# PE transposes for the first tile of each batch, the first two tiles in lockstep, and a fixed step table for attention from tile 4 on

## The chip, the cores and the metric

The kernel runs on one core of a Trainium2 chip. The core has TensorE (PE, matmuls, with PEld for the loading of weights into the array), VectorE (DVE), ScalarE (ACT), GpSimd (POOL) and SyncE (SP, which here issues every DMA), 16 DMA engines, the on-chip memory SBUF, and PSUM, where TensorE leaves its results. The metric is device time of one execution in microseconds (us). Three runs of the kernel before took 695.65, 696.09 and 697.74 us; their median is 696.09.

## The reference

Four batches of 768 tokens, 8 heads of 64. Attention sees the first 8 keys of a sequence (global) and the last 96 (local); a feed-forward block with layer norm follows, and its input is added to its output.

```python
scores = scale * np.matmul(q, k.transpose(0, 1, 3, 2))
is_global = pos[None, :] < int(n_global)
is_local = (rel >= 0) & (rel < int(n_local))
dist = np.where(is_global & ~is_local, float(n_local), np.abs(rel))
scores = np.where(is_global | is_local, scores - slopes * dist, -1e9)
a = np.exp(scores - max); a = a / (a.sum() + 1e-9)
x = np.matmul(a, v)                        # then (4, 768, 512)
xn = (x - mu) / np.sqrt(var + 1e-06) * g_ln
out = x + np.maximum(xn @ w_ch1, 0.0) @ w_ch2
```

The two weight matrices are 512x2048 and 2048x512, and they lie in memory as eight-byte floating-point words.

## The kernel before

**Numbers in two halves.** A value in four bytes is split into a high and a low two-byte half; a product is summed from three matmuls (high by high, high by low, low by high), scores from all four halves' products. `ffn1` (L330 to L332) and `product2` (L344) show it, and so do the three matmuls of pv (L259 to L261). The eight-byte weights are turned into two halves on the chip by `weight` (L144 to L157): three ACT and three DVE operations for each of 16 pieces of 1 MB, with three `st` buffers for the pieces.

**Tiles.** The 3072 tokens are 24 tiles of 128 tokens. `TILES` (L49) puts the first tile of each batch ahead: tiles 0 to 3 are first tiles of batches 3, 2, 1, 0; tiles 4 to 8 the rest of batch 0, and so on. A first tile attends only to itself (one block of 128 keys); any other attends to itself and the block ahead of it, into whose first 16 columns the global keys are copied (L215, L216). Two tiles form a chunk for the feed-forward part (`CT` = 2, twelve chunks).

**One tile's attention** (`attention`, L190) is a Python generator; its `yield`s are the places where other work may be traced in between. k, q and v are loaded into `ld` buffers (six of them) and split into halves. k (L180) and q (L202) are transposed by DMA; the halves of q change places for the cross products (L208; by DVE copies for tile 0, L206). Then come scores `s` (L234), masking with a row minimum (L239), the exponential (L243), the split of the result into `pn` (L246 on ACT for tiles 0 to 3, L248 on DVE after that, and L249 on POOL), its transpose by DMA (L251, `pT`, three buffers), pv with v (L259 to L261), the division (L265), the norm (`norm`, L269 to L282) and a last DMA transpose into `xT` (L282).

**PSUM.** Four pools of two banks: scores (`ps_s`), pv (`ps_v`), ffn1 (`ps_1`) and ffn2 (`ps_2`, tag `f2`).

**What sets the order.** The order on each engine is planned at compile time. The planner knows the data dependences and estimated durations; program order is the priority. `ORDER` and `mk` add some fixed edges by hand: a mark in the table waits in program order for another. Tile 0 is traced first, with the masks inside it; `run(f1w(), tokens(1), 0.6)` converts the first weight matrix, runs ffn1 of tile 0 alone (128 columns wide) and lets tile 1's generator advance 0.6 yields for each of its own. Tiles 1 to 3 follow likewise. Then `run(ffn(c), side, RATE)` goes through the chunks: for each step of the feed-forward part of chunk c, 1.6 yields of the attention of later tiles (`side`), one tile after another, up to one tile (`AHEAD`) past chunk c + 1.

Of the kernel before, what the change touches and what calls it, by code (L numbers as in the profile page):

```python
# [75 lines left out]
def banded(ctx, tc, q, k, v, n_global, n_local, g_ln, w1, w2, out, flag):  # L76
# [35 lines left out]

    def piece(src, name):
        st = p3.tile([P, 2, 512], I64, tag="st", name="st" + name, bufs=3)
        mk("D" + name, load.dma_start(out=st, in_=src))
# [28 lines left out]
    def weight(st, dh, dl, name, n):  # L144
# [6 lines left out]
        mk("A" + name, act.activation(out=lo, in_=st.rearrange("p a n -> p (a n)").bitcast(U32).rearrange("p (n two) -> p n two", two=2)[:, :, 0], func=AF.Relu, scale=2.0 ** -29, bias=less))  # L151
# [522 lines left out]
```

## Time and profile before

| what | value |
|---|---|
| median of three runs | 696.09 us (695.65 to 697.74) |
| span of the profiled execution, first to last instruction | 697.8 us |
| instructions | 14209 |
| PE busy, share of the span | 596.8 us, 86% |
| DVE busy | 392.7 us, 56% |
| ACT busy | 291.9 us, 42% |
| POOL busy | 157.5 us, 23% |
| DMA: moved, mean rate | 93.30 MB, 134 GB/s |
| mean granted clock of TensorE | 0.971 |

The profiled execution has no time of its own beside its span; the three runs above are what it can be held against. Rows of a group read: line, engine, operation, output<-input by the program's names, partitions x elements and type, count | busy us, mean ns of one | idle time of the engine just before, and what ended most of it. Rows of busy time by stretch read: the stretch and its length, then for PE and PEld (or all five engines) busy us and the number of instructions, then the granted clock of TensorE, the busy share of the DMA engines and GB/s. Rows of waits read: engine, waiting output and line <- what it waited for: us in total, times, longest. Timeline rows start with start and duration. SPq is the queue of DMA issues.

### The profile page before, as it was taken

The page shows a single profiled execution, that of the slowest core. Times are in us where ns is not written, and L with a number is a line of the kernel's source. Part 1 is how long each engine was busy: PE and PEld are TensorE (multiplying, and loading weights), DVE is VectorE, ACT ScalarE, POOL GpSimd, SP SyncE. Part 2 cuts the span into 40 slices and gives each one's busy share as a digit, 9 for nine tenths or more (in the row PEclk, how much of TensorE's full clock was granted, in tenths as well). Part 3 has the DMA queues.
Part 4 walks back from the last instruction along what each step waited for, and adds up shares of the span by engine and source line. Part 5 has one row for each costly group of instructions (what it writes and reads, how often), then busy time and mean ns, then how long its engine had stood idle before and what let it go on. Part 6 is the DMA issues. An engine that isn't in the chain of part 4 may idle for free. (4 is left out here: it accounts for less than half of the span.)

```text
span 697.8 us, 14209 instructions
## 1 busy us (share of the span) xinstructions
PE 596.8 (86%) x5602; PEld 426.6 (61%) x5602; DVE 392.7 (56%) x976; ACT 291.9 (42%) x752; POOL 157.5 (23%) x141
## 2 busy tenths in 40 slices
PE   0107698998499988999999999899989999999995
PEld 0106576775377576587496586496576586694762
DVE  4887978725567777565456456365445456342111
ACT  4886959323424442354254254253243254140110
POOL 0111304213213313332221331222231232120000
PEclk9999799999599999999999999999999999999999
DMA  9999999936888766676948746856853855231001
GB/s 230 221 278 262 237 260 187 172 58 115 163 161 143 129 139 136 134 148 117 178 90 151 140 96 134 150 106 123 159 118 73 151 82 94 69 62 31 16 1 36
DMA packets 264731, 93.30 MB, mean 134 GB/s; under 512 B 254416, under 2 KB 254416, under 8 KB 264656
## 3 DMA queue, kind: packets, MB, share of 16 engines
q1 hardware_dynamic: 264656, 92.31, 65.2%
q8 instruction: 46, 0.75, 0.5%
q14 instruction: 29, 0.24, 0.1%
HBM read 37.23 MB, written 6.29 MB: 62 GB/s over the span
## 5 line engine op out<-in xcount | busy, mean ns | idle before, releaser
L344 PE MATMUL f<-w2h,h_None 128*128 128x512 f16 x640 | 197.0, 380 | 0.0
L330 PE MATMUL f_None<-xT,w1h 128*128 128x256 f16 x640 | 176.1, 275 | 2.9 <-DVE h_None L336 2.4
L331 PE MATMUL f_None<-xT,w1h 128*128 128x256 f16 x640 | 176.1, 275 | 0.0
L332 PE MATMUL f_None<-xT,w1l 128*128 128x256 f16 x640 | 175.9, 275 | 0.0
L249 POOL TENSOR_TENSOR pn<-T,pn 128x512 f16<-128x512 f32 x88 | 109.2, 1243 | 218.2 <-DVE pn L248 111.6
L344 PEld LDWEIGHTS <-h_None 128*128 128x128 f16 x960 | 91.9, 98 | 99.7 <-issue 1.6
L344 PE MATMUL f<-w2l,h_None 128*128 128x512 f16 x320 | 121.8, 381 | 0.0
L331 PEld LDWEIGHTS <-w1h 128*128 128x128 f16 x896 | 90.7, 101 | 28.6 <-issue 19.0
L330 PEld LDWEIGHTS <-w1h 128*128 128x128 f16 x896 | 90.8, 101 | 16.5 <-DMA xT<-xn 6.9
L332 PEld LDWEIGHTS <-w1l 128*128 128x128 f16 x896 | 90.8, 101 | 7.6
L243 ACT ACTIVATE T<-T,mn 128x256 f32<-128x256 f32 (+1 forms) x192 | 92.4, 484 | 3.6
L335 ACT ACTIVATE h_None<-f_None 128x512 f16<-128x512 f32 x80 | 47.2, 592 | 107.1 <-PE f_None L332 107.0
L336 DVE SCALAR_TENSOR_TENSOR h_None<-f_None,h_None 128x512 f16<-128x512 f32 x80 | 54.7, 684 | 50.8 <-ACT h_None L335 50.8
L239 DVE CUSTOM_DVE_ANT_0 T<-s,mask 128x256 f32<-128x256 f32 (+1 forms) x192 | 67.1, 396 | 25.5 <-PE s L234 25.0
L234 PE MATMUL s<-kT,qT 128*128 128x128 f16 x704 | 55.2, 226 | 25.5 <-DMA qT<-qn 14.2
L259 PE MATMUL pv<-vn,pT 128*128 128x64 f16 x352 | 40.9, 196 | 39.9 <-DMA pT<-pn 39.8
L234 PEld LDWEIGHTS <-qT 128*128 128x128 f16 x704 | 47.4, 101 | 34.6 <-DMA qT<-qn 14.3
L330 PE MATMUL f<-xT,w1h 128*128 128x128 f16 x256 | 50.4, 237 | 17.1 <-DMA xT<-xn 17.1
L248 DVE CAST pn<-T 128x512 f16<-128x512 f32 x80 | 39.9, 502 | 42.8 <-ACT T L243 39.0
L259 PEld LDWEIGHTS <-pT 128*128 128x128 f16 x352 | 32.4, 99 | 50.1 <-DMA pT<-pn 47.9
L178 POOL TENSOR_TENSOR kn<-kf,kn 128x512 f16<-128x512 f32 x20 | 25.5, 1273 | 121.0 <-ACT kn L177 121.0
L276 POOL TENSOR_TENSOR rs<-rs,half 128x1 f32<-128x1 f32 x24 | 22.4, 931 | 133.5 <-DVE rs L275 133.5
(96 smaller groups left out, 804.0 us busy)
## 6 DMA issues: line engine op xcount, KB each, us to landing
st<-in_moe_w_ch_dram SPq DMA_DIRECT2D x16, 1024.0 KB, 7.4
vf<-in_v_dram SPq DMA_DIRECT2D x27, 256.0 KB, 3.6
kf<-in_k_dram SPq DMA_DIRECT2D x26, 256.0 KB, 3.8
qf<-in_q_dram SPq DMA_DIRECT2D x24, 256.0 KB, 3.3
out_dram<-x SPq DMA_DIRECT2D x24, 256.0 KB, 2.4
qT<-qT SPq DMA_DIRECT2D x46, 128.0 KB, 2.4
pT<-pn SPq DMA_TRANSPOSE x88, 3.3
kT<-kn SPq DMA_TRANSPOSE x27, 4.1
```

The costliest lines, as they stand in the source:

```text
L234: last = chain(last, pe.matmul(ps[:, u, n_ * P:(n_ + 1) * P], lhsT=qT[:, a * H + h, :], rhs=use[n_][0][:, h, :], start=(a == 0), stop=(a = ...
L239: vec.tensor_tensor_reduce(out=T[:, u, :], in0=ps[:, u], in1=mask, scale=1.0 / Z, scalar=3e38, op0=ALU.add, op1=ALU.min, accum_out=nm[:, h ...
L243: mk(f"e{t}_{g}", act.activation(out=T[:, u, :], in_=T[:, u, :], func=AF.Exp, scale=-1.0, bias=mn[:, h:h + 1], accum_out=sm[:, h:h + 1]))
L248: vec.tensor_copy(out=pn[:, :, 0, :], in_=T)
L249: pool.tensor_tensor(out=pn[:, :, 1, :], in0=T, in1=pn[:, :, 0, :], op=ALU.subtract)
L259: last = chain(last, pe.matmul(pv[:, h, :], lhsT=ph, rhs=vv[:, h, :D], start=(n_ == 0), stop=False))
L330: last = chain(last, pe.matmul(ps[:, a], lhsT=w1h[:, kk, fs], rhs=xT[:, kk, cols], start=(kk == 0), stop=False))
L331: last = chain(last, pe.matmul(ps[:, a], lhsT=w1h[:, kk, fs], rhs=xT[:, NK + kk, cols], start=False, stop=False))
L332: last = chain(last, pe.matmul(ps[:, a], lhsT=w1l[:, kk, fs], rhs=xT[:, kk, cols], start=False, stop=(kk == NK - 1)))
L335: mk("h" + key, act.activation(out=hh[:, 0], in_=ps, func=AF.Relu))
L336: mk("l" + key, vec.scalar_tensor_tensor(out=hh[:, 1], in0=ps, scalar=0.0, in1=hh[:, 0], op0=ALU.max, op1=ALU.subtract))
L344: pe.matmul(ps, lhsT=hh[:, a, :], rhs=w, start=(f == 0 and n_ == 0), stop=(f == NF - 1 and n_ == 2))
```

## The change

A new generator `first` does tiles 0 to 3. k and q stay in four-byte words as loaded; TensorE transposes them in four pieces of 128x128 against an identity matrix into a bank of `ps_2` (`flip`), and ACT and DVE split the result into halves straight out of PSUM (`split`). The same is done with the exponentials ahead of pv and with the normed x ahead of `xT`, so that no DMA transposes stand in these tiles. Heads 2j and 2j+1 share a transposed piece, in its upper and lower 64 partitions, and scores are taken over 64 partitions with four matmuls a head. The keys of a batch's first tile are loaded and transposed by DMA once more where tile 1 of the batch needs them, for all four batches now.

Tiles 0 and 1 are traced in lockstep (`pair`), with all six loads at the very start, and then tiles 2 and 3 in lockstep with the conversion of the first weight matrix and ffn1 of chunk 0. ffn1 is always 256 columns wide. ffn1 of chunk 1 is traced with the conversion of the second matrix, then ffn2 of tiles 0 and 1, then of 2 and 3.

From tile 4 on a table takes the place of the rate: `begin` gives each tile a step, eight steps from tile to tile, and `step` is called once for each step of the feed-forward part. A tile loads k, q and v in its step 0, splits and transposes q in 2, swaps q's halves in 4, takes scores in 6, 8, 10 and 12, and pv `LAG` = 4 steps after its scores, in 10, 12, 14 and 16. Two tiles are under way at a time. The hand-made edges (`ORDER`, `mk`) are gone. `pT` has four buffers instead of three; `mask0` and the identity matrix take `h` buffers.

```diff
-AHEAD = 1
-RATE = 1.6
+STEP = 8
+LAG = 4
...
-ORDER = {"D1_0_1": "q0", "L1": "q0", "L2": "p0_1", "L3": "p1_1"}
-ORDER.update({f"X{n}": f"l{2 + n // 8}_{2 * n % 16}" for n in range(16)})
...
-    early = {name: fetch(src, name, *TILES[0]) for name, src in (("k", k), ("q", q))}
+    early = {(name, t): fetch(src, name, *TILES[t]) for t in range(CT) for name, src in (("k", k), ("q", q), ("v", v))}
...
-    mask0 = const.tile([P, H, P], BF16, name="mask0")
+    mask0 = hpool.tile([P, H, P], BF16, tag="h", name="mask0")
     mask1 = const.tile([P, H, 2, P], BF16, name="mask1")
+    ident = hpool.tile([P, P], F32, tag="h", name="eye")
+    make_identity(nc, ident)
...
-        (pool if i else vec).tensor_tensor(out=kn[:, :, D:], in0=kf, in1=kn[:, :, :D], op=ALU.subtract)
+        pool.tensor_tensor(out=kn[:, :, D:], in0=kf, in1=kn[:, :, :D], op=ALU.subtract)
...
+    def flip(src, name):
+        ps = ps_2.tile([P, 4, P], F32, tag="f2", name=name)
+        for j in range(4):
+            pe.transpose(ps[:, j, :], src[:, j * P:(j + 1) * P], ident)
+        return ps
+    def split(ps, hi, lo, scale):
+        act.activation(out=hi, in_=ps, func=AF.Copy, scale=scale)
+        if scale == 1.0:
+            vec.tensor_tensor(out=lo, in0=ps, in1=hi, op=ALU.subtract)
+        else:
+            vec.scalar_tensor_tensor(out=lo, in0=ps, scalar=scale, in1=hi, op0=ALU.mult, op1=ALU.subtract)
+    def smalls():
+        return [p2.tile([P, H], F32, name=n_) for n_ in ("nm", "mn", "sm", "r")]
+    def row(pv, vv, h, n_, nb, ph, pl, last):
+        last = chain(last, pe.matmul(pv[:, h, :], lhsT=ph, rhs=vv[:, h, :D], start=(n_ == 0), stop=False))
+        last = chain(last, pe.matmul(pv[:, h, :], lhsT=ph, rhs=vv[:, h, D:], start=False, stop=False))
+        return chain(last, pe.matmul(pv[:, h, :], lhsT=pl, rhs=vv[:, h, :D], start=False, stop=(n_ == nb - 1)))
+    def quotient(pv, sm, r, x):
+        vec.tensor_scalar(out=r, in0=sm, scalar1=PS * 1e-9, scalar2=VS, op0=ALU.add, op1=ALU.mult)
+        vec.reciprocal(out=r, in_=r)
+        vec.tensor_tensor(out=x, in0=pv, in1=r.unsqueeze(2).to_broadcast([P, H, D]), op=ALU.mult)
+    def first(t, x, xT, at):
+        b, _ = TILES[t]
+        raw = [early[name, t] if (name, t) in early else fetch(src, name, b, 0) for name, src in (("k", k), ("q", q), ("v", v))]
+        yield
+        sides = []
+        for src, name, scale in ((raw[0], "k", 1.0), (raw[1], "q", -QS)):
+            d = p2.tile([P, 2, 4, P], F16, tag="kT0" if name == "k" else "qT", name=f"{name}0_{t}")
+            split(flip(src.rearrange("p h d -> p (h d)"), f"{name}t{t}"), d[:, 0], d[:, 1], scale)
+            sides.append(d)
+        kT, qT = sides
+        yield
+        vn = values(b, 0, raw[2])
+        firsts[b] = vn
+        nm, mn, sm, r = smalls()
+        parts = []
+        for e in range(2):
+            yield
+            T = p2.tile([P, 4, P], F32, tag="T", name=f"T{t}_{e}", bufs=3)
+            ps = ps_s.tile([P, 4, P], F32, tag="s", name=f"s{t}_{e}")
+            side = slice(e * D, (e + 1) * D)
+            last = None
+            for j in range(4):
+                for n_, (a, c) in enumerate(((0, 0), (0, 1), (1, 0), (1, 1))):
+                    last = chain(last, pe.matmul(ps[:, j, :], lhsT=qT[side, a, j, :], rhs=kT[side, c, j, :], start=(n_ == 0), stop=(n_ == 3)))
+            for j in range(4):
+                h = 2 * j + e
+                vec.tensor_tensor_reduce(out=T[:, j, :], in0=ps[:, j], in1=mask0[:, h], scale=1.0 / Z, scalar=3e38, op0=ALU.add, op1=ALU.min, accum_out=nm[:, h:h + 1])
+            act.activation(out=mn[:, e::2], in_=nm[:, e::2], func=AF.Copy, bias=LN_PS)
+            for j in range(4):
+                h = 2 * j + e
+                act.activation(out=T[:, j, :], in_=T[:, j, :], func=AF.Exp, scale=-1.0, bias=mn[:, h:h + 1], accum_out=sm[:, h:h + 1])
+            parts.append(T)
+        last = None
+        for e, T in enumerate(parts):
+            yield
+            pT = p2.tile([P, 2, 4, P], F16, tag="pT", name=f"pT{t}_{e}", bufs=LAG)
+            split(flip(T.rearrange("p j w -> p (j w)"), f"pt{t}_{e}"), pT[:, 0], pT[:, 1], 1.0)
+            if e == 0:
+                pv = ps_v.tile([P, H, D], F32, tag="pv", name=f"pv{t}")
+            for j in range(4):
+                last = row(pv, vn, 2 * j + e, 0, 1, pT[:, 0, j, :], pT[:, 1, j, :], last)
+        yield
+        quotient(pv, sm, r, x)
+        rs = moments(t, x)
+        xs = p2.tile([P, DM], F32, tag="T", name=f"xs{t}", bufs=3)
+        vec.tensor_scalar(out=xs, in0=x.rearrange("p h d -> p (h d)"), scalar1=mv[:, t, 0:1], scalar2=rs, op0=ALU.subtract, op1=ALU.mult)
+        vec.tensor_mul(out=xs, in0=xs, in1=gb)
+        yield
+        cols = slice(at * P, (at + 1) * P)
+        split(flip(xs, f"xt{t}"), xT[:, :NK, cols], xT[:, NK:, cols], 1.0)
+    firsts = {}
...
-        if i == 1 and b:
-            blocks[b, 0] = keys(b, 0), values(b, 0)
-            yield
         kT = keys(b, i)
-        qf = early["q"] if t == 0 else fetch(q, "q", b, i)
-        yield
+        qf = fetch(q, "q", b, i)
+        vf = fetch(v, "v", b, i)
+        if i == 1:
+            blocks[b, 0] = keys(b, 0), (firsts[b] if b == 0 else values(b, 0))
+        yield 2
         qn = p2.tile([P, H, P], F16, tag="ld", name=f"qn{t}", bufs=6)
         act.activation(out=qn[:, :, :D], in_=qf, func=AF.Copy, scale=-QS)
         vec.scalar_tensor_tensor(out=qn[:, :, D:], in0=qf, scalar=-QS, in1=qn[:, :, :D], op0=ALU.mult, op1=ALU.subtract)
         qT = p2.tile([P, 2 * H, P], F16, name="qT")
-        mk(f"q{t}", sp.dma_start_transpose(out=qT[:, :H, :], in_=qn.rearrange("p h d -> p (h d)")))
-        yield
+        sp.dma_start_transpose(out=qT[:, :H, :], in_=qn.rearrange("p h d -> p (h d)"))
+        vn = values(b, i, vf)
+        blocks[b, i] = kT, vn
+        yield 4
         for here, there in ((slice(0, D), slice(D, P)), (slice(D, P), slice(0, D))):
-            if t == 0:
-                vec.tensor_copy(out=qT[here, H:, :], in_=qT[there, :H, :])
-            else:
-                load.dma_start(out=qT[here, H:, :], in_=qT[there, :H, :])
-        yield
-        vn = values(b, i)
-        blocks[b, i] = kT, vn
+            load.dma_start(out=qT[here, H:, :], in_=qT[there, :H, :])
+        yield 6
...
+        pTs, last, pv = {}, None, None
+        for step in range(6, 13 + LAG):
+            if i > 1 and step == 5 + LAG:
+                vec.tensor_copy(out=vp[:GK], in_=vg[:GK])
+            g, odd = divmod(step - 6, 2)
+            if not odd and g < H // gh:
+                T = p2.tile([P, gh, W], F32, tag="T", name=f"T{t}_{g}", bufs=3)
+                ps = ps_s.tile([P, gh, W], F32, tag="s", name=f"s{t}_{g}")
...
+                pTs[g] = p2.tile([P, gh * 2 * nb, P], F16, tag="pT", name=f"pT{t}_{g}", bufs=LAG)
+                sp.dma_start_transpose(out=pTs[g], in_=pn.rearrange("p j a w -> p (j a w)"))
+            g, odd = divmod(step - 6 - LAG, 2)
+            if not odd and g >= 0:
+                pT = pTs.pop(g)
+                for u in range(gh):
+                    h = g * gh + u
+                    if h == 0:
+                        pv = ps_v.tile([P, H, D], F32, tag="pv", name=f"pv{t}")
+                    for n_ in range(nb):
+                        last = row(pv, use[n_][1], h, n_, nb, pT[:, (u * 2) * nb + n_, :], pT[:, (u * 2 + 1) * nb + n_, :], last)
+            yield step + 1
+        quotient(pv, sm, r, x)
...
-        yield from attention(t, xs[t], xTs[c], at)
+        yield from (attention if TILES[t][1] else first)(t, xs[t], xTs[c], at)
...
-    def ffn1(c, f, t=None):
-        n, cols = (CT * P, slice(0, CT * P)) if t is None else (P, slice(t % CT * P, (t % CT + 1) * P))
+    def ffn1(c, f):
+        n = CT * P
...
-            if f % 4 == 3 and f < NF - 1:
+            if (f + 1) * len(ts) % 4 == 0 and f < NF - 1:
...
+    def ffn_due(j, c_):
+        if c_:
+            ffn1(0, 4 * j)
+            ffn1(0, 4 * j + 2)
...
-    one = tokens(0)
-    for _ in range(4):
-        next(one)
-    build_masks()
-    go(one)
-    build_mask1()
-    run(f1w(), tokens(1), 0.6)
-    run(f1(1), tokens(2), 2.0)
-    run(f1(2), tokens(3), 2.0)
-    run(f2w(), f1(3), 0.5)
...
-    run(seq(ffn2(0, 1), ffn2(2), ffn2(3)), side(3 * CT + AHEAD), RATE)
-    for c in range(2, NC):
-        g = side((c + 2) * CT + AHEAD)
-        run(ffn(c), extremes(g) if c == 3 else g, RATE)
...
+    pair = both(tokens(0), tokens(1))
+    next(pair)
+    build_masks()
+    go(pair)
+    build_mask1()
+    begin = {t: 7 * (t - 2 * CT) if t < 6 else STEP * (t - 7) + 23 for t in range(2 * CT, B * NT)}
+    live, now, t_next = [], 0, 2 * CT
+    def step():
+        nonlocal now, t_next
+        while t_next in begin and begin[t_next] <= now:
+            live.append([now, t_next, tokens(t_next)])
+            t_next += 1
+        for g in list(live):
+            while g[0] <= now:
+                at = next(g[2], None)
+                if at is None:
+                    live.remove(g)
+                    break
+                g[0] = begin[g[1]] + at
+        now += 1
+    def run(main, *others):
+        for _ in main:
+            step()
+            for g in others:
+                next(g, None)
+    half1 = both(f1w(), tokens(2), tokens(3))
+    go(itertools.islice(half1, 4))
+    run(half1)
+    run(blocks1(1), f2w())
+    run(ffn2(0, 1))
+    run(ffn2(2, 3))
+    run(ffn(2))
+    run(ffn(3), extremes())
+    for c in range(4, NC):
+        run(ffn(c))
```

`smalls`, `row`, `quotient` and `moments` hold lines of the old `attention` and `norm` unchanged.

More of the change, by code (lines that the diff above doesn't have):

```diff
@@ L160, in weights1 @@
         sl, cs = slice(j * 512, (j + 1) * 512), slice(2 * c, 2 * c + 2)
-        weight(piece1(j, c) if j or c else early["w"], w1h[:, cs, sl], w1l[:, cs, sl], f"1_{j}_{c}", 2 * j + c)
+        weight(piece1(j, c), w1h[:, cs, sl], w1l[:, cs, sl], f"1_{j}_{c}", 2 * j + c)
     def weights2(f):
@@ L215, in attention @@
             vec.tensor_copy(out=kp[:, :, :GK], in_=kg[:, :, :GK])
-            vec.tensor_copy(out=vp[:GK], in_=vg[:GK])
-        use = [blocks[b, j] for j in range(max(i - 1, 0), i + 1)]
-        nb = len(use)
+        use = [blocks[b, i - 1], blocks[b, i]]
+        nb, gh = 2, 2
         W = nb * P
-        gh = 4 // nb
-        nm = p2.tile([P, H], F32, name="nm")
-        mn = p2.tile([P, H], F32, name="mn")
-        sm = p2.tile([P, H], F32, name="sm")
-        r = p2.tile([P, H], F32, name="r")
@@ L329, in ffn1 @@
             for kk in range(NK):
-                last = chain(last, pe.matmul(ps[:, a], lhsT=w1h[:, kk, fs], rhs=xT[:, kk, cols], start=(kk == 0), stop=False))
-                last = chain(last, pe.matmul(ps[:, a], lhsT=w1h[:, kk, fs], rhs=xT[:, NK + kk, cols], start=False, stop=False))
-                last = chain(last, pe.matmul(ps[:, a], lhsT=w1l[:, kk, fs], rhs=xT[:, kk, cols], start=False, stop=(kk == NK - 1)))
-        hh = hpool.tile([P, 2, m, n], F16, tag="h", name=f"h{c}_{t}_{f}")
-        key = f"{c}_{f}" if t is None else f"t{t}_{f}"
-        mk("h" + key, act.activation(out=hh[:, 0], in_=ps, func=AF.Relu))
-        mk("l" + key, vec.scalar_tensor_tensor(out=hh[:, 1], in0=ps, scalar=0.0, in1=hh[:, 0], op0=ALU.max, op1=ALU.subtract))
+                last = chain(last, pe.matmul(ps[:, a], lhsT=w1h[:, kk, fs], rhs=xT[:, kk, :], start=(kk == 0), stop=False))
+                last = chain(last, pe.matmul(ps[:, a], lhsT=w1h[:, kk, fs], rhs=xT[:, NK + kk, :], start=False, stop=False))
+                last = chain(last, pe.matmul(ps[:, a], lhsT=w1l[:, kk, fs], rhs=xT[:, kk, :], start=False, stop=(kk == NK - 1)))
+        hh = hpool.tile([P, 2, m, n], F16, tag="h", name=f"h{c}_{f}")
+        act.activation(out=hh[:, 0], in_=ps, func=AF.Relu)
+        vec.scalar_tensor_tensor(out=hh[:, 1], in0=ps, scalar=0.0, in1=hh[:, 0], op0=ALU.max, op1=ALU.subtract)
         for a in range(m):
-            for u in range(n // P):
-                hs[c * CT + u if t is None else t, f + a] = hh[:, :, a, u * P:(u + 1) * P]
+            for u in range(CT):
+                hs[c * CT + u, f + a] = hh[:, :, a, u * P:(u + 1) * P]
     def product2(ps, t, f):
@@ L361, in ffn2, with blocks1 @@
         yield
-    def ffn(c):
+    def blocks1(c):
         for f in range(0, NF, 2):
@@ L366, in ffn @@
             yield
+    def ffn(c):
+        yield from blocks1(c)
         for n_ in range(CT):
             yield from ffn2(c * CT + n_)
-    def run(main, side, rate):
-        due = 0.0
-        for _ in main:
-            due += rate
-            while due >= 1.0:
-                due -= 1.0
-                next(side, None)
-        for _ in side:
-            pass
     def seq(*gens):
@@ L390, in both, with go @@
             yield
-    def f1(t):
-        for f in range(0, NF, 4):
-            ffn1(t // CT, f, t)
-            yield
+    def go(g):
+        for _ in g:
+            pass
     def f1w():
@@ L408, in f2w, with extremes @@
             yield
[L410 to L433 removed]
+    def extremes():
         for n_ in range(16):
```

109 lines of the change are left out of this document (34 added, 75 removed).

## The prediction

> **What bounds the kernel now.** I read the engine shares first, then what TensorE did stage by stage, then who kept it waiting.
>
> ```profile
> PE 596.8 (86%) x5602; PEld 426.6 (61%) x5602; DVE 392.7 (56%) x976; ACT 291.9 (42%) x752; POOL 157.5 (23%) x141
> ```
>
> TensorE (PE) is the busiest, but that figure counts overlapping matmuls up to their modelled ends. The useful number is the pitch: start to start, back to back. From the chain of waits and the timeline (start, duration, what):
>
> ```profile
> 585.34 0.45 PE s L234 x8
> 627.77 20.72 PE f L344 x96
> 612.76 0.27 PE L331 MATMUL f_None<-xT,w1h 128*128 128x256 f16 x1
> ...
> 613.85 0.27 PE L332 MATMUL f_None<-xT,w1l 128*128 128x256 f16 x1
> 440.42 0.19 PE L259 MATMUL pv<-vn,pT 128*128 128x64 f16 x1
> ...
> 440.74 0.19 PE L261 MATMUL pv<-vn,pT 128*128 128x64 f16 x1
> ```
>
> So 128 columns cost 0.45/8 = 0.056 us, 512 columns 20.72/96 = 0.216, 256 columns (613.85 - 612.76)/10 = 0.109, a 64-column pv matmul (440.74 - 440.42)/11 = 0.029. Ffn1 in the head is narrow (a group of the same line), and the rest of the counts come from one view of busy time by stretch for each of L330 (L331 and L332 are as many), L344, L234 and L259 (L260 and L261 as many), in this order:
>
> ```profile
> L330 PE MATMUL f<-xT,w1h 128*128 128x128 f16 x256 | 50.4, 237 | 17.1 <-DMA xT<-xn 17.1
> ...
> 0.00:200.00 200.00, 56.67 (x276) 29.95 (x277) 0.92 0.91 198
> 200.00:640.00 440.00, 152.37 (x556) 54.58 (x556) 0.99 0.63 120
> 640.00:697.80 57.80, 17.45 (x64) 6.26 (x64) 0.97 0.05 19
> ...
> 0.00:200.00 200.00, 44.09 (x192) 18.20 (x192) 0.92 0.91 198
> 200.00:640.00 440.00, 188.84 (x826) 78.83 (x827) 0.99 0.63 120
> 640.00:697.80 57.80, 30.03 (x136) 13.04 (x134) 0.97 0.05 19
> ...
> 0.00:200.00 200.00, 15.68 (x168) 12.58 (x168) 0.92 0.91 198
> 200.00:640.00 440.00, 39.55 (x536) 34.78 (x536) 0.99 0.63 120
> ...
> 0.00:200.00 200.00, 9.53 (x76) 7.38 (x76) 0.92 0.91 198
> 200.00:640.00 440.00, 31.34 (x276) 25.07 (x276) 0.99 0.63 120
> ```
>
> So of the first 276, 256 are 128 columns wide and 20 are 256 wide. Pure work up to 200 us: 256 x 3 x 0.0556 + 20 x 3 x 0.109 + 192 x 0.216 + 168 x 0.0556 + 76 x 3 x 0.029 = 42.7 + 6.5 + 41.4 + 9.3 + 6.6 = 106.6, so **93.4 us are lost in the head**. From 200 to 640: 181.8 + 178.3 + 29.8 + 24.0 = 413.9, **26.1 lost**. After 640: 20.9 + 29.3 = 50.2, **7.6 lost**. Work 570.7 plus 127.1 lost is the span, 697.8. No row tells what lies around the span; it stands 1.7 us above the 696.09 median of the runs, and I subtract that 1.7 at the end.
>
> What the losses wait for: TensorE's waits up to 200 us, then from 200 to 640 (the last line).
>
> ```profile
> PE pv L259 <- DMA pT<-pn: 24.1, 10, 11.8
> PE f L330 <- DMA xT<-xn: 17.1, 4, 15.5
> PE s L234 <- DMA qT<-qn: 14.2, 2, 13.8
> PE f L344 <- ACT w2h L156: 6.4, 2, 4.0
> PE s L234 <- DVE nm L239: 4.1, 1, 4.1
> ...
> PE pv L259 <- DMA pT<-pn: 15.7, 18, 2.5
> ```
>
> Transposed tiles dominate, but behind them in the head stands VectorE (DVE), busy 100 of the 125 us until the last weight piece is split:
>
> ```profile
> 0.00:125.00 125.00, 63.15 (x733) 51.17 (x734) 100.08 (x196) 93.11 (x186) 24.09 (x23) 0.95 1.01 237
> L157 DVE TENSOR_TENSOR w2l<-st,w2h x8: 1170/1216/2183, 74.7 to 123.4; 128x1024 f16<-128x1024 f32 x8
> 10.08 0.17 DVE L66 CAST nf<-nn 128x4 f32<-128x4 int32 x1 [3.59 <-DMA nn<-in_n_local_dram]
> ```
>
> **The change part by part.** Prices come from these groups (busy, mean ns), the landing time of pT, L336's count up to 125 us and four timeline rows:
>
> ```profile
> L336 DVE SCALAR_TENSOR_TENSOR h_None<-f_None,h_None 128x512 f16<-128x512 f32 x80 | 54.7, 684 | 50.8 <-ACT h_None L335 50.8
> L265 DVE TENSOR_TENSOR x<-pv,r 128x512 f32<-128x512 f32 x24 | 16.5, 689 | 60.7 <-PE pv L261 59.8 <-DMA qT<-qT 0.9
> L239 DVE CUSTOM_DVE_ANT_0 T<-s,mask 128x256 f32<-128x256 f32 x160 | 60.1, 419 | 25.5 <-PE s L234 25.0 <-POOL pn L249 0.4
> L248 DVE CAST pn<-T 128x512 f16<-128x512 f32 x80 | 39.9, 502 | 42.8 <-ACT T L243 39.0 <-DMA pT<-pn 1.7 <-DMA xT<-xn 1.7
> L249 POOL TENSOR_TENSOR pn<-T,pn 128x512 f16<-128x512 f32 x88 | 109.2, 1243 | 218.2 <-DVE pn L248 111.6 <-issue 44.4 <-ACT pn L246 39.4
> L206 DVE COPY qT<-qT 64x1024 f16<-64x1024 f16 x2 | 0.8, 422 | 0.0
> pT<-pn SPq DMA_TRANSPOSE x88, 3.3
> 0.00:125.00 125.00, 6.12 (x9) 0.95 1.01 237
> 1.88 0.99 SPq L115 DMA_DIRECT2D st<-in_moe_w_ch_dram  x1
> 16.21 1.67 PE L234 MATMUL s<-kT,qT 128*128 128x128 f16 x14 [2.02 <-DVE qT L206]
> 5.53 3.85 SPq L180 DMA_TRANSPOSE kT<-kn  x1
> 9.71 1.20 ACT L151 ACTIVATE st<-st,less 128x1024 int32<-128x1024 uint32 x1 [3.94 <-DMA st<-in_moe_w_ch_dram]
> ```
>
> *TensorE's own work.* Chunks 0 and 1 run 384 matmuls of 256 columns instead of 768 of 128: 41.9 - 42.7 = -0.8. A first tile's scores take 16 matmuls per half instead of 8: 64 more, +3.6. Work is 570.7 - 0.8 + 3.6 = 573.5.
>
> *The 80 transposes* (20 in each of tiles 0 to 3) have no row. Below: a warm 128-column matmul, 0.056. Above: twice a cold one, 2 x 1.67/14 = 0.24. I take the cold 0.12, the nearest row, since TensorE stands nearly idle there: 20 x 0.12 = 2.4 us on a tile's path. They replace, on a first tile, four DMA steps in a row (kT and qT, pT, xT), of which the first alone held the queue 3.85 us. The pair's path then has DVE and ACT as links; I put its end at some 38 us: the counts land at 10; then DVE has two tiles with some ten operations of 0.68 each, 14 us, and I allow as much again for the waits on ACT and for weight work between them. This number is rough, and the next part shows that it decides little: 30 us of slack.
>
> *DVE until the last weight piece.* Before: 100.1. Added: eight pT splits that were ACT and POOL work, out of PSUM like L336, 8 x 0.68 = 5.5; one more operation for xs in each first tile, between nothing (two short ones for L279) and 0.69 as L265, taken at 0.69 x 4 = 2.8; all 16 h blocks instead of 9 by then, 7 x 0.68 = 4.8; tile 4's scores, which start in the table's step 6 while w2 is converted, 8 x 0.42 + 4 x 0.50 = 5.4. Removed: the two qT copies, 0.8. Sum 117.8. With the same 25 us of idle time w2 ends at 143; with only some 8 us of it, while the first inputs and the counts land, at 126. I take 135. By then TensorE can have done ffn1 of both chunks (41.9), scores and pv of tiles 0 to 4 (160 x 0.0556 + 144 x 0.029 = 13.1) and 7/8 of the first ffn2 pair (18.1): 73.1. It starts ffn1 at 38 and has 97 us for the remaining 65, so the pair's chain could end 30 us later at no cost. Lost: 135 - 73 = 62; bounds 53 and 70. What is late next was, before, attention of tiles 4 and 5 (4.1 us behind nm, 24.1 behind pT). Now tile 5 ends in step 24 and chunk 2 begins in step 29, five steps of 2.6 us later (12 matmuls of 0.216). For the rest of the join I take 4 us, between 0 and 9. Head: **66**, instead of 93.4.
>
> *pv four steps behind.* A step holds at least 2.6 us of ffn work, four of them 10.4; pn, pT and the landing take about 1.2 on POOL, as much on the queue and 3.3 to land. So the 15.7 us of pT waits go, and nothing takes their place if the queue keeps up: 26.1 - 15.7 = **10.4**. The price without that cover is the 15.7 again.
>
> *Moved queues.* SP loses 19 transposes (kT 27 to 24, qT 24 to 20, pT 88 to 80, xT 24 to 20) and six qT copies and gains one k load. Six early loads now stand ahead of the counts and of the first weight piece, issued at 1.9 us now; with the counts, gs and gb some eight entries pass it, at half to one microsecond each (its own took 0.99): 4 to 8 us later. DVE has masks and splits meanwhile; without that cover the shift is the cost, inside the bounds above. POOL gains an identity matrix, under 1 us beside the 10 us wait for the counts, and four kn in place of DVE's seven, which nothing waits for in the table's first two steps.
>
> *New waits.* The pair needs four T tiles in three buffers, and all flips share two PSUM banks with ffn2: each flip waits for the split two before it, on DVE. Behind a waiting flip on TensorE stand only the other tile's scores, behind the reductions on DVE a weight operation of 1.2 us. It lies in the slack.
>
> *Tail*: unchanged, 7.6.
>
> **Sum:** 573.5 + 66 + 10.4 + 7.6 = 657.5 of span, minus 1.7: **656 us**, own range 643 to 672 (head 53 to 79, steady 7 to 15).
>
> **Rivals.**
>
> 1. *The compile-time planner pulls pv forward again*, so that the table's lag does not show: the steady waits stay, 656 + 15.7 = 672. For it: order in the program is only a priority. Against: with ffn work always ready, later program order means later in the queue. 0.10.
> 2. *The first ffn2 pair takes both banks before tile 3's flips.* xT of tile 3 then waits for all of w2, and ffn1 of chunk 1, 21 us, follows instead of being hidden: 677. It needs the first w2 piece split before tile 3's last flip; in the old trace that split starts only at 74.7. 0.08.
> 3. *The head gains nothing*: DVE's extra work pushes w2 to 150 or later, and tiles 4 and 5 are late as before. Head 93: 697.8 + 2.8 - 15.7 - 1.7 = 683. DVE at 80% busy speaks for it, the idle 25 us against. 0.11.
> 4. *A cold TensorE becomes the head's bound.* At 16.2 us the trace shows 0.12 for 128 columns, twice the warm pitch, and the granted clock up to 200 us is 0.92. If all 65 us from 38 on ran at half pace they would need 130 instead of 97: 656 + 33 = 689. The work comes in bursts, so a part will, not all. 0.05. By the Trainium skill (TensorE: Matmul & The Clock Gate, "HAM oscillation — how this bites in real kernels"), an idle window of about 3.4 us puts the clock back to half; the old head's gaps of 11.8 to 15.5 us followed by the cold pitch agree.
> 5. *Slower: the queue of SP breaks the lag.* Two tiles are in flight, each with up to eight users of the six ld buffers; SP works in order, so one load that waits for a buffer holds the other tile's pT. It decides once a pT is over four steps late. One landing of 3.3 us per tile lost on TensorE, 20 tiles: 656 + 66 = 722; from 2 us per tile on it eats the gain. The old queue's longest sum of waits, over the whole span, was this:
>
> ```profile
> SPq L251 <- POOL pn L249: 65.3, 44, 6.4
> ```
>
>    and TensorE still lost only 26 us in the steady part. 0.06.
>
> **How the numbers follow.** Forecast 0.60, rivals 0.10, 0.08, 0.11, 0.05, 0.06. The likeliest gives 656. The range 640 to 686 holds the forecast and rivals 1 to 3 and leaves out rival 4, rival 5 and the ends. About 0.3% (2 us) is what a measurement can tell from no change. Faster: all of the forecast and of rivals 1 to 3, and most of 4: 0.92. Slower: rival 5 and a little of the rest, 0.06. Same: 0.02.
>
> **What will show it.** Right: the last w2 split near 135 us; ffn1 of chunk 0 from about 38 us in 256 columns only; hardly any wait of pv on pT after 200 us; no gap of several us between 150 and 190; flips of 0.06 to 0.24 us. Wrong: a w2 end beyond 150 or before 120 (DVE mis-sized), an early ffn2 that stands ahead of tile 3's flips, pT waits over 10 us in the steady part, or SP waiting for loads with pv behind it.

## The result, and the profile after

The changed kernel takes 705.43 us, median of four runs (703.16 to 709.42), against 696.91 us (695.65 to 700.80) before: a ratio of 1.0117, 95% interval 1.0072 to 1.0162. It is slower, by 1.2%; 656 us had been forecast. The profiled execution took 703.98 us, with a span of 702.2.

The first row is the page's line of engine shares. Then, for the kernel after, busy time by stretch of one line at a time: ffn1 (L391; L392 and L393 are as many), ffn2 (L404), scores of a first tile (L228), scores of the others (L299), pv (L195; two more lines are as many). The columns are the stretch, its length, PE busy us and number of matmuls, granted clock, DMA share, GB/s.

```profile
PE 609.9 (87%) x5362; PEld 432.8 (62%) x5362; DVE 386.4 (55%) x983; ACT 292.0 (42%) x753; POOL 146.0 (21%) x139
```

```profile
0.00:140.00 140.00, 19.07 (x64) 0.89 0.71 188
140.00:200.00 60.00, 17.29 (x64) 0.96 0.44 89
200.00:640.00 440.00, 157.16 (x576) 1.00 0.65 125
640.00:702.20 62.20, 17.45 (x64) 0.96 0.07 23
...
0.00:140.00 140.00, 0.00 (x0) 0.89 0.71 188
140.00:200.00 60.00, 33.66 (x142) 0.96 0.44 89
200.00:640.00 440.00, 193.04 (x858) 1.00 0.65 125
640.00:702.20 62.20, 34.19 (x155) 0.96 0.07 23
...
0.00:140.00 140.00, 12.17 (x128) 0.89 0.71 188
...
0.00:140.00 140.00, 2.95 (x24) 0.89 0.71 188
140.00:200.00 60.00, 4.72 (x56) 0.96 0.44 89
200.00:640.00 440.00, 45.21 (x560) 1.00 0.65 125
...
0.00:140.00 140.00, 5.43 (x32) 0.89 0.71 188
140.00:200.00 60.00, 3.75 (x32) 0.96 0.44 89
200.00:640.00 440.00, 33.66 (x288) 1.00 0.65 125
```

With the prediction's pitches (0.327 for three matmuls of 256 columns, 0.216, 0.056, 0.087 for three of pv; the new transposes count as no work) the work is 32.2 us up to 140 us, 57.5 from there to 200, 429.8 to 640 and 54.4 behind. So TensorE lost 107.8, 2.5, 10.2 and 7.8 us. Counted in the same way the kernel before lost 74.9 up to 140 us, 17.9 to 200, 26.0 to 640. **The steady part came out as forecast, and the gap between 140 and 200 us is gone; the whole failure lies ahead of 140 us**, where not one matmul of ffn2 ran (x0). TensorE's waits up to 200 us, and then from 200 to 640 (the last two rows):

```profile
PE xt L180 <- DVE xs L251: 40.1, 4, 18.9
PE pv L197 <- DVE pT L187: 5.8, 3, 4.2
PE pv L195 <- ACT pT L185: 5.2, 4, 3.4
...
PE f L391 <- DVE h L396: 6.3, 8, 2.4
PE pv L195 <- DMA pT<-pn: 1.9, 2, 1.3
```

Before, TensorE waited here for DMA transposes. Now four waits hold 40.1 us: the transposes of normed x into `xT`, one for each first tile. What they wait for shows in the timeline of DVE, and the last two of them in that of PE (start, duration, what, and in brackets the idle time ahead):

```profile
38.74 2.34 DVE L470 TENSOR_REDUCE wm<-w1h 128x1 f32<-128x1024 f16 x2
40.99 0.68 DVE L202 TENSOR_TENSOR x<-pv,r 128x512 f32<-128x512 f32 x1
...
46.25 1.22 DVE L138 SCALAR_TENSOR_TENSOR st<-st 128x1024 int32<-128x1024 int32 x1
47.38 0.69 DVE L173 SCALAR_TENSOR_TENSOR vn<-vf,vn 128x512 f16<-128x512 f32 x1
47.98 1.22 DVE L143 TENSOR_TENSOR w1l<-st,w1h 128x1024 f16<-128x1024 f32 x1
49.12 2.35 DVE L470 TENSOR_REDUCE wm<-w1h 128x1 f32<-128x1024 f16 x2
51.37 0.18 DVE L329 BATCH_NORM_AGGREGATE mv<-st 128x2 f32<-128x6 f32 x1
...
58.67 0.69 DVE L251 TENSOR_TENSOR xs<-xs,gb 128x512 f32<-128x512 f32 x1
```

```profile
135.97 1.09 PE L180 MATMUL xt<-eye,xs 128*128 128x128 f32 x4 [18.88 <-DVE xs L251]
...
139.97 1.09 PE L180 MATMUL xt<-eye,xs 128*128 128x128 f32 x4 [1.95 <-DVE xs L251]
...
141.71 0.63 PE L404 MATMUL f<-w2h,h 128*128 128x512 f16 x1
```

From x of tile 0 at 41.0 to the end of its xs at 59.4 the norm's own operations are a few of 0.2 to 0.7 us; of the rest of those 18 us some 12 are ten weight operations and reduces of 1.2 us each that stand ahead of them in DVE's order, and most of what is left is the same kind of short operation for tile 1. Tiles 2 and 3 repeat it, and ffn2 starts behind the last of their transposes.

Where the reduces went, DVE up to the last weight piece, and that piece:

```profile
L470 DVE TENSOR_REDUCE wm<-w1h x8: 1211/1216/1219, 38.7 to 79.0; 128x1 f32<-128x1024 f16 x8
L470 DVE TENSOR_REDUCE wm<-w2h x8: 1211/1214/1218, 83.0 to 138.0; 128x1 f32<-128x1024 f16 x8
...
0.00:138.00 138.00, 63.59 (x516) 50.01 (x516) 117.16 (x233) 94.64 (x192) 13.37 (x21) 0.90 0.73 191
...
L143 DVE TENSOR_TENSOR w2l<-st,w2h x8: 1197/1218/1222, 81.9 to 136.9; 128x1024 f16<-128x1024 f32 x8
```

The sixteen reduces (19.4 us) ran at 195 to 280 us before; without their edges the planner put them into the conversion. The last piece is split at 136.9 to 138.1.

### The profile page after: what moved, and what is told of

It reads as the page before. It is cut to its first block, busy times and chain, and to the rows that moved or that the text cites. A ratio compares the mean times of both kernels' runs of the same rounds, so it can differ in the third digit from the quotient of the medians.

```text
span 702.2 us, 13689 instructions
## 1 busy us (share of the span) xinstructions
PE 609.9 (87%) x5362; PEld 432.8 (62%) x5362; DVE 386.4 (55%) x983; ACT 292.0 (42%) x753; POOL 146.0 (21%) x139
## 5 line engine op out<-in xcount | busy, mean ns | idle before, releaser
L404 PE MATMUL f<-w2h,h 128*128 128x512 f16 x768 | 238.8, 381 | 0.0
L391 PE MATMUL f<-xT,w1h 128*128 128x256 f16 x768 | 211.0, 275 | 9.3 <-DVE h L396 8.9
L392 PE MATMUL f<-xT,w1h 128*128 128x256 f16 x768 | 211.0, 275 | 0.0
L393 PE MATMUL f<-xT,w1l 128*128 128x256 f16 x768 | 211.0, 275 | 0.0
L404 PEld LDWEIGHTS <-h 128*128 128x128 f16 x1152 | 110.4, 98 | 121.9 <-issue 1.6
L404 PE MATMUL f<-w2l,h 128*128 128x512 f16 x384 | 146.2, 381 | 0.0
L396 DVE SCALAR_TENSOR_TENSOR h<-f,h 128x512 f16<-128x512 f32 x96 | 65.8, 686 | 75.9 <-ACT h L395 75.7
L395 ACT ACTIVATE h<-f 128x512 f16<-128x512 f32 x96 | 56.3, 590 | 100.8 <-PE f L393 98.4
L303 DVE CUSTOM_DVE_ANT_0 T<-s,mask 128x256 f32<-128x256 f32 x160 | 60.9, 417 | 61.0 <-PE s L299 61.0
L391 PEld LDWEIGHTS <-w1h 128*128 128x128 f16 x768 | 75.8, 99 | 17.2 <-DVE h L396 5.0
L392 PEld LDWEIGHTS <-w1h 128*128 128x128 f16 x768 | 75.7, 99 | 16.5 <-issue 6.1
L307 ACT ACTIVATE T<-T,mn 128x256 f32<-128x256 f32 x160 | 79.9, 500 | 4.1
L393 PEld LDWEIGHTS <-w1l 128*128 128x128 f16 x768 | 75.8, 99 | 9.3
L309 DVE CAST pn<-T 128x512 f16<-128x512 f32 x80 | 34.2, 427 | 68.5 <-ACT T L307 65.7
L304 ACT ACTIVATE mn<-nm 128x2 f32<-128x2 f32 x80 | 16.1, 201 | 123.4 <-DVE nm L303 123.4
L299 PE MATMUL s<-kT,qT 128*128 128x128 f16 x640 | 52.9, 224 | 4.6 <-DMA qT<-qT 2.8
L195 PE MATMUL pv<-vn,pT 128*128 128x64 f16 x352 | 42.8, 196 | 7.1 <-ACT pT L185 5.2
L299 PEld LDWEIGHTS <-qT 128*128 128x128 f16 x640 | 41.9, 100 | 10.7 <-DMA qT<-qT 2.9
L197 PE MATMUL pv<-vn,pT 128*128 128x64 f16 x352 | 41.5, 196 | 5.8 <-DVE pT L187 5.8
L196 PE MATMUL pv<-vn,pT 128*128 128x64 f16 x352 | 42.7, 196 | 0.0
```

The source lines that it names most:

```text
L195: last = chain(last, pe.matmul(pv[:, h, :], lhsT=ph, rhs=vv[:, h, :D], start=(n_ == 0), stop=False))
L196: last = chain(last, pe.matmul(pv[:, h, :], lhsT=ph, rhs=vv[:, h, D:], start=False, stop=False))
L299: prev = chain(prev, pe.matmul(ps[:, u, n_ * P:(n_ + 1) * P], lhsT=qT[:, a * H + h, :], rhs=use[n_][0][:, h, :], start=(a == 0), stop=(a = ...
L303: vec.tensor_tensor_reduce(out=T[:, u, :], in0=ps[:, u], in1=mask1[:, h].rearrange("p n w -> p (n w)"), scale=1.0 / Z, scalar=3e38, op0=AL ...
L307: act.activation(out=T[:, u, :], in_=T[:, u, :], func=AF.Exp, scale=-1.0, bias=mn[:, h:h + 1], accum_out=sm[:, h:h + 1])
L391: last = chain(last, pe.matmul(ps[:, a], lhsT=w1h[:, kk, fs], rhs=xT[:, kk, :], start=(kk == 0), stop=False))
```

## The experiments

The twelve kernels with a part put back, taken alone or moved are in one table: median, ratio to the runs of the kernel before on the same chip with its 95% interval, and what TensorE lost by stretch in the one profiled execution of each, counted as above.

| kernel | us | ratio (interval) | lost 0-60 | 60-140 | 140-200 | 200-640 |
|---|---|---|---|---|---|---|
| before | 696.9 | 1 | 55.0 | 19.8 | 17.9 | 26.0 |
| after | 705.4 | 1.0117 (1.0072-1.0162) | 55.0 | 52.8 | 2.5 | 10.2 |
| e4: old head, table | 675.0 | 0.9688 (0.9627-0.9749) | 54.7 | 24.2 | 3.4 | 11.5 |
| e8: new head, old steady part | 730.5 | 1.0462 (1.0386-1.0538) | 55.0 | 51.5 | 1.5 | 37.8 |
| e5: e4, pv one step behind | 691.8 | 0.9888 (0.9824-0.9951) | 55.7 | 22.3 | 6.3 | 28.7 |
| e6: before, no reduce edges | 710.1 | 1.0147 (1.0077-1.0217) | 56.4 | 27.9 | 15.3 | 32.4 |
| e1: after, reduce edges back | 690.8 | 0.9896 (0.9865-0.9927) | 55.0 | 38.7 | 0 | 16.1 |
| e3: after, flips in score banks | 690.1 | 0.9862 (0.9824-0.9900) | 55.0 | 33.3 | 5.9 | 11.7 |
| e2_hold_w1: e1, w1 held | 682.8 | 0.9777 (0.9727-0.9828) | 49.8 | 33.5 | 1.6 | 14.3 |
| e2b_hold_only: after, w1 and w2 held | 682.2 | 0.9770 (0.9732-0.9809) | 48.9 | 35.0 | 3.5 | 10.4 |
| e2_hold: e1, w1 and w2 held | 680.0 | 0.9758 (0.9702-0.9814) | 49.1 | 28.2 | 4.5 | 13.5 |
| e7: e2_hold, flips in score banks | 678.4 | 0.9709 (0.9649-0.9769) | 48.8 | 28.3 | 3.3 | 13.0 |
| e12: e7, all of w1 held | 680.8 | 0.9780 (0.9737-0.9824) | 48.0 | 31.8 | 2.9 | 14.8 |
| e10: e4, half of w1 held | 677.7 | 0.9703 (0.9663-0.9743) | 51.2 | 22.3 | 9.9 | 11.5 |

**The two halves of the change, apart (e4, e8).** The core of e4's driver, with `attention` of before for tiles 0 to 3 and that of after (`later`) for the rest; e8 is the reverse. The hand-made edges go with the old head: e4 has them, and e8 has none, so that their loss counts to the new head here. e4 also leaves ffn2 of tiles 2 and 3 one after the other.

```diff
-        yield from attention(t, xs[t], xTs[c], at)
+        yield from (later if TILES[t][1] else attention)(t, xs[t], xTs[c], at)
...
-    run(f1(2), tokens(3), 2.0)
-    run(f2w(), f1(3), 0.5)
+    run(stepped(f1(2)), tokens(3), 2.0)
+    run(stepped(f2w()), f1(3), 0.5)
```

> The other part of the change alone: the head of the kernel before (DMA transposes, tiles 0 to 3 one after another, its hand-made edges), and from tile 4 on the table with pv four steps behind, four pT buffers. If the two parts are independent: 696.9 less the 16 us that PE lost more in 200 to 640 (26.1 against 10.2) and less the 16 us in 140 to 200 (18.1 against 2): 665 us. If the gain in 140 to 200 belongs to the new head: 681. If the head of before, with attention of tiles 4 and 5 started beneath it by the table, is crowded on DVE: 685 to 695.

> The other half of the split: the head of after as it stands (tiles 0 to 3 in pairs, transposes by PE, no edges) with the steady part of before (attention of tiles 4 on by the rate of 1.6 yields a step, pv right behind its scores, three pT buffers). If the two parts of the change add up: 705.4 + 697.6 - 675.0 = 728 us, PE losing about 107 by 140 us and 26 more in 200 to 640. If what the table gains in 140 to 200 is gained only behind the head of before: 712.

The halves multiply: 0.9688 x 1.0462 = 1.0136, and both together gave 1.0117. The table brings 3.1%, 22 us; the new head, edges included, costs 4.6%, some 32 us. Of e4's gain, 14.5 us lie in 200 to 640 and 14.5 in 140 to 200, and the head up to 140 gives 4 back: the gap of tiles 4 and 5 closes by the table and needs no new head. That is 10 us short of the sum I had expected: 4 are the head, 3 the two gains being 14.5 instead of 16, and the rest would lie between single spans and medians.

**The lag (e5).**

```diff
-LAG = 4
+LAG = 1
```

> The run of the table alone (head of before, 675.0 us) with one number changed: pv is traced one step behind its scores instead of four (four pT buffers stay). Theory L (the lag takes the waits of pv for pT, as the prediction had it): most of the 15.7 us of pT waits come back, 685 to 691 us, and pv <- DMA pT stands in PE's waits from 200 to 640 with 10 us or more. Theory E (the even spacing of the tiles and the fourth buffer do it, the planner moves pv behind other work anyway): within 3 us of 675.

The number of `pT` buffers stays at four. TensorE's waits from 200 to 640 us, first in e4, then in e5:

```profile
PE pv L273 <- DMA pT<-pn: 6.7, 4, 2.1
...
PE pv L273 <- DMA pT<-pn: 19.3, 24, 2.7
```

The waits are back, 24 of them instead of 4, and the time with them: 16.8 us. It is the lag, not the even spacing.

**The reduces' edges (e1, e6).** In e1 the lost edges are put back into after; in e6 the same sixteen are taken out of before.

```diff
+ORDER.update({f"X{n}": f"l{2 + n // 8}_{2 * n % 16}" for n in range(16)})
```

> The kernel after, with one thing put back: the sixteen hand-made edges that hold the reduce of each weight piece (L470, 16 x 1.215 = 19.4 us on DVE) until the chunks behind the head. Theory A (the lost edges): DVE sets the head's end, so all 19.4 us come back: 705.4 - 19.4 = 686 us, last w2l near 119, loss of PE in 0 to 200 down from 110 to 91. Theory B (the order on DVE's queue: the norms of tiles 0 and 1, and of 2 and 3, stand among weight operations of 1.2 us each): only the reduces that stand between x and xs matter, 4 of them (4.9 us) for tiles 0 and 1 and 4 (4.9 us) for tiles 2 and 3: 696 us at best, ffn1 of chunk 0 still starts near 61. Theory C (the reduces only fill time in which DVE waits for ACT and for the pieces): no difference, 703 to 708.

> The kernel before, less the sixteen edges that hold the reduces of the weights back; nothing else. Theory A (the edges are what the new head lacked, whatever the head): the planner draws the reduces into the conversion here too, w2's conversion ends up to 19.4 us later, and the time is 8 to 15 us longer: 705 to 712. Rival (the head of before waits for DMA transposes and not for DVE, so the reduces fill gaps): within 3 us of 697.

Both moved: 14.6 us less in the new head, 10 to 13 us more in the old one. In e6 w2's last piece starts at 129.7 us instead of 123.4, so only a third of the 19.4 us reached the end of the conversion:

```profile
L156 DVE TENSOR_TENSOR w2l<-st,w2h x8: 1211/1217/2065, 75.9 to 129.7; 128x1024 f16<-128x1024 f32 x8
```

The loss is larger than that delay. About half of it, 6.4 us, lies from 200 to 640 us, behind the last reduce (131.6); no run says why. For the part in the head the next runs but one suggest the order on DVE. e1 lies between the two theories, 691 against 686 and 696; its last piece of w2 starts at 125.2 us instead of 136.9, where theory A had 119.

**The banks (e3).**

```diff
-        ps = ps_2.tile([P, 4, P], F32, tag="f2", name=name)
+        ps = ps_s.tile([P, 4, P], F32, tag="s", name=name)
```

> The kernel after with one edit: the flips in the score banks in place of the ffn2 banks; reduces and weights as in after. Theory F (the flips of tiles 2 and 3, queued ahead of ffn2 in its own banks, keep ffn2 of tiles 0 and 1 from the gap of 19 us at 117 to 136): ffn2 starts near 120 instead of 142 and 10 to 15 us go, 690 to 695. Theory G (w2l itself ends at 138 on DVE, so ffn2 could use little of the gap): 702 to 706.

The transposes of x in e3, and then ffn2 by stretch in e3:

```profile
L180 PE MATMUL xt<-eye,xs x16: 272/346/447, 58.6 to 141.0; 128*128 128x128 f32 x16
...
0.00:140.00 140.00, 26.12 (x95) 0.94 0.73 188
```

The last transpose of x is as late as in after (141.0), the reduces are where they were, and yet the time falls by 15 us: 95 matmuls of ffn2, 20.5 us of work, now run ahead of 140 us in TensorE's idle time, from 77.9 us on (I had expected some 120), where after has none. With one pair of banks for both, the two ffn2 accumulations hold both banks until all of w2 is there, so it is either the transposes first or ffn2 first, and the planner had put the transposes first.

**The order on DVE (e2_hold_w1, e2_hold, e2b_hold_only).** The first DVE operation of a weight piece waits, in DVE's order, for the normed x: w1's pieces 2 to 7 for that of tile 1, w2's for that of tile 3. e2b_hold_only has these edges without those of the reduces.

```diff
+ORDER.update({f"W{n}": "x1" for n in range(2, 8)})
+ORDER.update({f"W{n}": "x3" for n in range(8, 16)})
```

> The reduces held as in the run before, and two ops more held on DVE: the work of w1's pieces 2 to 7 starts behind the normed x of tile 1. Theory A: the weights bound the head, so what the norms gain (x at 41, xs at 59; the chain alone is some 7 us) the weights lose on the same engine: same as the run before within 3 us. Theory B (order): xs of tile 1 by about 48 instead of 63, ffn1 of chunk 0 from about 51 instead of 66, and 10 to 15 us off the time of the run before. It could also be slower: ffn1 then runs dry waiting for w1l, as pieces 2 to 7 need 6 x 3.7 = 22 us of DVE from 48 on.

> As the run before, and w2's pieces held on DVE behind the normed x of tile 3. Theory A: w2's end is what the head waits for, so a later start of w2 makes it slower than the run before, by up to 10 us. Theory B: ffn1 of chunk 1 is the work that PE lacks between 117 and 140, and w2 is converted beneath it (8 x 3.7 = 29 us of DVE beneath 38 us of ffn1): 15 us off the run before, ffn1 of chunk 1 from about 110 instead of 141.

> The kernel after with the weights held behind the norms (w1's pieces 2 to 7 behind tile 1, w2's behind tile 3) and the reduces left free. If edges and order add up: 705.4 - 10.8 = 695 us (10.8 is what the holding brought where the reduces were held too). If the holding alone cures it, since the planner then finds no gap for the reduces ahead of the norms: 680 to 686. If the planner now draws all sixteen reduces into the freed gaps ahead of the norms: 700 or more.

The group of the transposes of x in e1, e2_hold_w1 and e2b_hold_only, in this order (count | busy, mean ns | idle ahead of it and why), and where e2b_hold_only has its reduces:

```profile
L189 PE MATMUL xt<-eye,xs 128*128 128x128 f32 x16 | 4.3, 427 | 30.1 <-DVE xs L260 30.1
```

```profile
L190 PE MATMUL xt<-eye,xs 128*128 128x128 f32 x16 | 4.3, 425 | 18.5 <-DVE xs L261 18.5
```

```profile
L190 PE MATMUL xt<-eye,xs 128*128 128x128 f32 x16 | 4.1, 425 | 6.3 <-DVE xs L261 6.3
...
L480 DVE TENSOR_REDUCE wm<-w1h x8: 1204/1206/1214, 54.8 to 92.6; 128x1 f32<-128x1024 f16 x8
L480 DVE TENSOR_REDUCE wm<-w2h x8: 1199/1206/1212, 118.7 to 160.4; 128x1 f32<-128x1024 f16 x8
```

Holding w1 took 8 us off e1, ffn1 of chunk 0 starting at 47.9 us instead of 62.1. The step to holding w2 as well (2.8 us) is inside the intervals; the 15 us that theory B expected did not come. The telling run is e2b_hold_only: all its reduces still run by 162 us, those of w1 from 54.8 to 93.8 in the middle of the head, yet the time is that of e2_hold within the intervals. They are not free: up to 140 us TensorE loses some 6 us more than in e2_hold, and it gets 3 back from 200 to 640, since e2_hold has its reduces from 190 us on. But none of them stands between a tile's x and its xs, and so DVE's load alone was not what cost 14.6 us in e1. **In these runs reduces and weight operations cost most where they stand between x and the end of a norm; elsewhere most of their time lies beneath ffn1.** Theory A falls in the form in which I put it.

**Both cures together (e7), and nothing ahead of the pair (e12).** e7 is e2_hold with e3's edit; e12 holds pieces 0 and 1 of w1 as well (`range(8)` in the first edge).

> The run with the reduces and both weights held (680.0 us), and the flips put into the score banks in place of the two ffn2 banks. Theory F (flips and the ffn2 pair exclude each other in two banks, so ffn2 of tiles 0 and 1 can't fill the gaps before the last flip): 4 to 8 us off, 672 to 676, with ffn2 before the last xt flip. Rival S (the flips now wait for scores of tiles 4 and 5 in the same banks): 680 to 686. Neither: within 2 us of 680.

> The new head with reduces held, flips in score banks and both weights held (678.4 us), and now pieces 0 and 1 of w1 held on DVE behind the normed x of tile 1 too, so that nothing of the weights stands in DVE's queue ahead of the first pair. Question: was the prediction's 38 us for the pair's chain right for the chain alone? Theory P (yes): the pair's chain loses the 7.4 us of six weight operations that stand in it, flips of x at 36 to 38 instead of 42.8. For the time: theory A (DVE has no slack in the head, so work shifted behind the pair comes back one for one): 678 to 684, as ffn1 then waits for w1l. Theory B (the start of ffn1 decides): 672 to 676.

e7 can't be told from e2_hold. Edges, holding and banks bring 15, 23 and 15 us taken alone and 27 together: they overlap, as cures of one stall do. In e12 the pair's transposes of x come at 39.0 us, by the timeline of PE:

```profile
38.98 1.30 PE L191 MATMUL xt<-eye,xs 128*128 128x128 f32 x5 [6.32 <-DVE xs L262]
```

So up to these transposes the chain of the pair takes 39 us when no weight work stands in it. That they start 4 us earlier than in e7 (42.8) brought nothing: ffn1 starts at 46.7 us instead of 47.1. The held weight operations now follow the last xs at once, three of them (39.4 to 42.8) ahead of DVE's first split of `xT`, and the first matmul starts when the high half of w1 is written (46.7).

**The same order in the old head (e10).** e4, with w1's pieces 4 to 7 held behind the normed x of tile 0.

> The table with the head of before (675.0 us), and four edges of the kind that helped the new head: the work of w1's pieces 4 to 7 on DVE starts behind the normed x of tile 0. Theory B (order on DVE's queue, whatever the head): x of tile 0 at 39.7, xn ended at 49.5 in that run, its own operations being 4 us; xn 4 to 5 us earlier, ffn1 of tile 0 from about 51 instead of 55.8, and 3 to 5 us off: 670 to 672. Rival (this head waits for DMA transposes, and w1's later end takes back what tile 0 gains): 673 to 678.

No gain: xn came 4.7 us earlier (48.7 to 44.0) and was taken back by w1, which TensorE now waits for:

```profile
PE f L409 <- DMA xT<-xn: 8.2, 1, 8.2
PE f L409 <- ACT w1h L157: 7.5, 1, 7.5
```

The best kernel of the study is **e4, the table with the old head: 0.9688 (0.9627 to 0.9749) of before**, faster than both kernels. The repaired new head (e7) can't be told from it.

## Why the prediction was wrong, and where it was right

*TensorE's work*, forecast 573.5: counted 573.9. *Price of a transpose*, taken at 0.12: four took 1.09 us cold and 0.64 warm (see below), a pitch of 0.12 to 0.22, inside the bounds. On the path of a tile, five times four of them, that is up to 5.5 us instead of 2.4.

*pv four steps behind*, 10.4 us left in 200 to 640: 10.2, and e5 shows that the lag does it. Rivals 1 and 5 did not occur; pT waits are 1.9 us. *Join*, 4 us, and tiles 4 and 5 no longer late: 2.5 us in 140 to 200. The prediction gave the table's steps as the reason but entered the gain under the head; e4 shows that the table alone brings it, with the old head.

*The pair's chain ends at 38*, with some weight work in it and ffn1 starting there: too early in every run. In after, the transposes of x came at 59.5 and 63.4 and ffn1 at 65.7, because of what stands in DVE's order. With no weight work in the chain (e12) the transposes came at 39.0, which is near 38 but is not what the 38 stood for, and ffn1 at 46.7. **"Behind the reductions on DVE a weight operation of 1.2 us. It lies in the slack" and "30 us of slack" are the sentences that failed first.** Not one operation of 1.2 us stood between x and xs of tile 0 but ten, two of them reduces. And the slack was not there: e2_hold_w1 started ffn1 14 us earlier than e1 and gained 8.

*DVE until the last weight piece*, 117.8 us of work and an end at 135: 117.2 and 138. Right by accident: 18 us of it are fifteen of the sixteen reduces, which the sum lacked, so its other terms were too high. Eight h blocks were done by then instead of sixteen (5.4 us less) and only two of the twelve operations for tile 4's scores (4.6 us less), because ffn1 of chunk 1 and tile 4 were late themselves. That the hand-made edges go stood in the change's description and had no price. It was worth 14.6 us (e1).

***"By then TensorE can have done ... 73.1"* is the step that decided.** Up to 140 us it did 32.2. The 73.1 held ffn1 of both chunks and 7/8 of the first ffn2 pair, as if they needed only the weights. Ffn1 of chunk 1 needs the normed x of tiles 2 and 3, and I never dated it: 135 and 139 us. Ffn2 needs two PSUM banks, and I had seen that the transposes share them, but looked only at ffn2 getting ahead of tile 3 (rival 2, which cost ffn1 of chunk 1). The mirror image happened: the transposes stood in the queue first and ffn2, 20.7 us, waited. e3 shows it with nothing else changed.

*Rival 3, the head gains nothing, 683*, comes near the time of the repaired new head, but not by its reasons: e7 lost 80.4 us up to 200, not 93, about what the old head loses with the table (e4, 82.3), and tiles 4 and 5 were not late. The forecast of 66 was not reached by any kernel. The 14 us that e7 still misses lie ahead of 60 us. With ffn1 dense from 38 on, TensorE would have lost 33 us there (38 less 5 of scores and pv, at the prediction's pitches); e7 lost 48.8, and every version of the new head with weights held 48 to 50. In e7 the transposes of x start at 42.8, and ffn1 with two matmuls at 47.1:

```profile
47.13 0.58 PE L402 MATMUL f<-xT,w1h 128*128 128x256 f16 x2 [2.43 <-ACT xT L196]
```

Its third matmul follows at 50.9, and the pace is half up to 54.3. The split of `xT` that it waits for stands behind a weight operation on ACT (45.4 to 46.6) and on DVE behind three (43.1 to 47.6): the holding has moved the weight work from before xs to the next link. No run takes it away there, so that this is the cause stays an argument.

*Rival 4*, the cold TensorE: seen, but short, see below. The gaps of the old head that the prediction names there lie ahead of TensorE's first warm stretch and can't show that idle time cools it; after does, with four transposes in 0.64 us at 110.5 and, behind the idle 18.9 us, in 1.09 at 136.0. *Slower* had been given 0.06, nearly all of it for rival 5, which did not occur. The own range of 643 to 672 is narrower than its bounds, which add up to 639 to 673; it decides nothing.

The Trainium skill (VectorE: DVE Perf Modes, "Rules for kernel authors") advises TensorE for a 128x128 transpose where PSUM is a good destination, otherwise DMA. For the operation alone this case agrees: the four transposes of an operand take 0.6 to 1.1 us on TensorE, where a DMA transpose of pT took 3.3 us to land. For the time no run sets the two kinds of transpose apart with all else equal; the whole repaired new head (e7) can't be told from the old one (e4). My reading, not shown by a run, is that the way out of PSUM takes back what the operation gains, an ACT and a DVE operation for each operand, and a bank.

## What to carry to other kernels

Before summing an engine's load, write down the order of its queue around every short operation that another engine waits for: a load that fits can still stand at the wrong place, and edges that hold work back have to be priced when they go. When two stages get the same PSUM banks, ask both ways round who is queued first and what the other could have done meanwhile. Cures that each bring 15 us for one stall don't add, so a change of two parts is worth splitting first.
